# A gated linear attention with a feed-forward layer on one core: outputs and late keys turned by DMA transposes, scores in 64-row tiles

## The chip, the cores and the metric

The kernel runs on one core of one Trainium2 chip. The metric is the device time of that core in microseconds. Eight runs of the kernel before have a median of 205.31 us (204.4 to 206.87).

## The reference

Four batches, eight heads, 768 positions and a head size of 48. With f = sigmoid(f_logit), every head keeps a 48 x 48 state:

```
for t in range(S):
    state = f[:, :, t, :, None] * state + outer(k[:, :, t], v[:, :, t])
    y[:, :, t] = q[:, :, t] @ state
x = y, heads side by side        # 3072 tokens x 384
h = x @ w_in                     # 384 x 2048
out = gelu(h) @ w_out            # 2048 x 384, exact gelu, float32
```

## The kernel before

**Chunks.** The 3072 tokens are cut into 24 chunks of 128 positions, six to a batch. Inside a chunk the decay is turned into factors: Exp and Ln on ACT (L403, L407) give log f, a triangular matmul sums it over positions (L424), and two Exp (L428, L432) give gt and rg. DVE multiplies kp = k * rg (L435) and qp = q * gt (L439), and GpSimd casts v into a padded tile vp (L449). A batch in the sense of the list BATCH is one to four chunks whose Exp and Ln are one instruction.

**Attention of a chunk (`attn`).** `keys` turns kp and qp with four TensorE transposes each into PSUM (L490). Two DVE copies place the keys in kb, a zero-padded tile in which each head of a pair has its own column block, so that a full 128-row matmul can multiply one head's keys with the pair's queries (L230 by way of `copy`); one ACT copy makes qT (L228). `scores` runs eight 128-column matmuls in two halves (L533), and DVE multiplies each half with the causal mask (L541). The state matmul (L581) has 96 columns per pair; DVE and GpSimd update the state (L596, L598, L604). The outputs are made already transposed, with features on partitions: eight matmuls of v against scores (L618) and, if there is a state, four of the state against qT (L622), all 128 columns. Four copies of the shapes 96 x 384 and 3 times 32 x 128 place them in xT, the input of the feed-forward layer. The first four chunks (NDB 2, "dbl") are loaded two at a time with two neighbouring positions on a partition, and have their own views.

**Feed-forward (`ffn_group`).** Chunks are taken in groups (SIZES, four or two chunks). The first layer (L664) uses 16 x 3 matmuls a group with w_in as weights, ACT does Gelu out of PSUM (L668), and the second layer (L681) has 16 matmuls of 384 columns a chunk, in four steps "F2.n.r" of four, step r using the r-th piece of w_out. ACT copies the result (L228) and SP stores it (L689).

**What sets the order.** The code collects all operations in a planner (`Plan`), with an engine, an estimated length, dependencies, ring buffers (`Ring`, `Buf`) and a priority (PRI); the planner places them greedily by earliest start, and the instructions are issued per engine in that order. Each engine works strictly through its list. An operation with an "alt" may go to another engine if its chunk is below ALTN. Loads, stores (and every other DMA of the plan) go through SP's one queue; the weights are cast and loaded through GpSimd's. ORDER fixes how the loads of chunks (c), w_in (W) and w_out (O) follow each other. LOCK and the gates separate Exp stretches from Gelu stretches on ACT, because a change of function table costs a load (L774). PSUM has eight banks: three hps (feed-forward), three aps (attention), two tp (transposes). In the first 26 us, gaps that the planner foresees on PE are filled with dummy matmuls (L755).

Of the kernel before, what the change touches and what calls it, by code (L numbers as in the profile page):

```python
# [8 lines left out]
F32 = mybir.dt.float32  # L9
BF16 = mybir.dt.bfloat16  # L10
# [4 lines left out]
class Ring:  # L15


    def __init__(self, bufs=0, make=None, fixed=None):
        self.bufs, self.make, self.fixed, self.order = bufs or len(fixed), make, fixed, []
        self.zero = None  # L20
# [5 lines left out]
class Buf:  # L26
# [3 lines left out]
    def ready(self):  # L30

        r = self.ring
        if self.slot is not None:
            return 0.0
        if len(r.order) < r.bufs:
            z = r.zero[len(r.order)] if r.zero else None
            return z.vis if z else 0.0
        old = r.order[len(r.order) - r.bufs]
        t = 0.0
        for u in old.users:  # L40
            if u.end is None:
                return None
            t = max(t, u.vis)
        return t
# [6 lines left out]
    def t(self):  # L51
        if self.handle is None:
            r = self.ring
            self.handle = r.fixed[self.slot] if r.fixed else r.make(**self.kw)
        return self.handle
# [10 lines left out]
class Plan:  # L66
# [34 lines left out]
    def run(self):  # L101
# [10 lines left out]
        while left:  # L112
            best, stay, cand = None, None, []
            for o in left:
                ok = True
                t0 = o.nb
                for b in o.bufs:
                    v = b.ready()
                    if v is None:
                        ok = False  # L120
                        break
                    t0 = max(t0, v)
# [41 lines left out]
def kernel(  # L164
# [12 lines left out]
    C = 128  # L177
# [9 lines left out]
    SIZES = [4, 2, 2, 4, 4, 4, 4]  # L187
    ORDER = ['c0', 'c1', 'W0', 'c2', 'c3', 'W1', 'c4', 'W2', 'c5', 'c6', 'W3', 'O0', 'O1', 'O2', 'O3']
# [3 lines left out]
    RMAJOR = 0  # L192
    LOCK = 4
    KBALT = 1
    ALTN = 4
    BIAS = 0
    PRI = {'F': 2, 'RG': 5, 'R': -2, 'GL': 2, 'Tk': 20, 'VC': -10, 'Y': 20, 'x': 2, 'QT': 10, 'C': -2, 'T': 2, 'O': -20, 'A': 2}
    QALTN = 0
    NDB = 2
    CRING = 1  # L200
    CEARLY = 3
    HPB, ASB = 3, 3
    BATCH = [2, 2, 1, 1, 2, 1, 1, 2, 4, 2, 1, 1, 2, 1, 1]
# [5 lines left out]
    ld = ctx.enter_context(tc.tile_pool(name="ld", bufs=6))  # L209
    ld2 = ctx.enter_context(tc.tile_pool(name="ld2", bufs=2))  # L210
    amp = ctx.enter_context(tc.tile_pool(name="amp", bufs=5))
    lg = ctx.enter_context(tc.tile_pool(name="lg", bufs=3))
    el = ctx.enter_context(tc.tile_pool(name="el", bufs=3))
    at = ctx.enter_context(tc.tile_pool(name="at", bufs=3))
    fx = ctx.enter_context(tc.tile_pool(name="fx", bufs=3))
    fg = ctx.enter_context(tc.tile_pool(name="fg", bufs=2))
    hp = ctx.enter_context(tc.tile_pool(name="hp", bufs=HPB, space=PSUM))
    asp = ctx.enter_context(tc.tile_pool(name="asp", bufs=ASB, space=PSUM))
    tpp = ctx.enter_context(tc.tile_pool(name="tpp", bufs=2, space=PSUM))
# [47 lines left out]
    NLF, NQ, NV, NKB = 2, 4, 6, 3  # L267
    lfs = [one.tile([C, 4, H, 64], BF16, name=f"lf{i}") for i in range(NLF)]
    qps = [one.tile([C, H, 64], BF16, name=f"qp{i}") for i in range(NQ)]
    kps = [one.tile([C, H, 64], BF16, name=f"kp{i}") for i in range(NQ)]  # L270
    vps = [one.tile([C, H * VB], BF16, name=f"vp{i}") for i in range(NV)]
    KBW = P2 * 2 * C + 64
    kbs = [one.tile([C, 2 * KBW], BF16, name=f"kb{i}") for i in range(NKB)]
# [27 lines left out]
    r_qp = padded(qps, "POOL", 0.2, zpad, -95)  # L301
    r_kp = padded(kps, "POOL", 0.2, zpad, -95)
    r_vp = padded(vps, "DVE", 0.65, zall, -99)
    r_kb = padded(kbs, "DVE", 1.2, zall, -93)
# [3 lines left out]
    r_fl = Ring(3, lambda: lg.tile([C, 4, H, D], F32, name="fl"))  # L308
    r_in = {n: Ring(6, lambda n=n: ld.tile([C, H, D], F32, name=n)) for n in ("qt", "kt", "vt")}
    r_gt = Ring(3, lambda: el.tile([C, H, D], F32, name="gt"))  # L310
    r_rg = Ring(3, lambda: el.tile([C, H, D], F32, name="rg"))
    r_gl = Ring(3, lambda: el.tile([C, 4, P2], F32, name="gl"))
    r_in2 = {n: Ring(2, lambda n=n: ld2.tile([C, H, 2 * D], F32, name=n + "2")) for n in ("qt", "kt", "vt")}
    r_qT2 = Ring(2, lambda: ld2.tile([C, P2, 2, C], BF16, name="qT2"))
    r_qT = Ring(3, lambda: at.tile([C, P2, C], BF16, name="qT"))
    r_am = Ring(5, lambda: amp.tile([C, 4, C], BF16, name="am"))
    r_rr = Ring(3, lambda: at.tile([C, P2, 2 * D], F32, name="rr"))
    r_tn = Ring(3, lambda: at.tile([C, P2, 2 * D], F32, name="tn"))
    r_xT = Ring(3, lambda: fx.tile([C, KO, 4 * C], BF16, name="xT"))
    r_os = Ring(3, lambda: fx.tile([C, d_model], F32, name="osb"))  # L320
    r_gT = Ring(2, lambda: fg.tile([C, FO * 4 * C], BF16, name="gT"))
    r_hp = Ring(HPB, lambda: hp.tile([C, 512], F32, name="hps"))
    r_as = Ring(ASB, lambda: asp.tile([C, 512], F32, name="aps"))
    r_tp = Ring(2, lambda: tpp.tile([C, P2, C], BF16, name="tp"))
# [26 lines left out]
    X = [{} for _ in range(NCH)]  # L351

# [38 lines left out]
    def stage1(g):  # L391
# [23 lines left out]
        for n in ns:  # L415
# [3 lines left out]
            x.update(qp=r_qp.new(), kp=r_kp.new(), vp=[r_vp.new() for _ in range(1 + dbl)])  # L419
            pr = 10 * n  # L420

            def cum(gps=gps, j=j):
# [13 lines left out]
                x["kp"].t()[:, :, 0:D], loaded(n, "kt"), rg.t(), ALU.mult),  # L436
                rd=[("rg", n), ("kt", n)], wr=[("kp", n)],
                bufs=[x["kp"], x["kt"], rg], prio=pr, name=f"KP{n}")
            P.add("DVE", 0.57, lambda x=x, gt=gt, n=n: eng().tensor_tensor(  # L439
                x["qp"].t()[:, :, 0:D], loaded(n, "qt"), gt.t(), ALU.mult),  # L440
                rd=[("gt", n), ("qt", n)], wr=[("qp", n)],
                bufs=[x["qp"], x["qt"], gt], prio=pr + 1, name=f"QP{n}",
                  alt=(("POOL", 0.9),) if n < QALTN else None)

            for a, vb in enumerate(x["vp"]):
                rows = slice(64 * a, 64 * a + 64) if dbl else slice(0, C)

                def cast(vb=vb, rows=rows, n=n):
                    nc.gpsimd.tensor_copy(vb.t()[rows].rearrange("p (h x) -> p h x", x=VB)[:, :, 0:D],  # L449
                                          loaded(n, "vt")[rows])  # L450
                P.add("POOL", 0.52, cast, rd=[("vt", n)],
                      wr=[("vp", n, a)], bufs=[vb, x["vt"]], prio=pr, name=f"VC{n}")
# [19 lines left out]
    def vwin(vp, h):  # L472
        o = h * VB - D * (h % 2)
        return vp[:, o:o + C]

    def keys(n):

        x, dbl = X[n], n < 2 * NDB
        qp, kp = x["qp"], x["kp"]
        tps = [r_tp.new(), r_tp.new()]  # L480
        kb = x["kb"] = r_kb.new()
        if dbl:
            qT = x["qT"] = X[n - 1]["qT"] if n % 2 else r_qT2.new()
        else:
            qT = x["qT"] = r_qT.new()
        pr = 10 * n

        def trans(i, src):
            for p in range(P2):
                nc.tensor.transpose(tps[i].t()[:, p, :], src.t()[:, 2 * p:2 * p + 2, :], ident)  # L490
        P.add("PE", 0.225, lambda: trans(0, kp), rd=[("kp", n), "ident"], wr=[("tk", n)], bufs=[tps[0], kp],
              prio=pr + 4, name=f"Tk{n}")
        P.add("PE", 0.225, lambda: trans(1, qp), rd=[("qp", n), "ident"], wr=[("tq", n)], bufs=[tps[1], qp],
              prio=pr + 4, name=f"Tq{n}")

        def block(hh):
            src = tps[0].t()[64 * hh:64 * hh + D]
            if dbl:
                w = kb.t()[64 * hh:64 * hh + D].rearrange("q (a x) -> q a x", a=2)[:, :, 0:P2 * 2 * C]
                w = w.rearrange("q a (p h c) -> q a p h c", p=P2, h=2)[:, :, :, hh, 0:64]  # L500
                copy(w, src.rearrange("q p (a c) -> q a p c", a=2))
            else:
                copy(kbv(kb, 0)[64 * hh:64 * hh + D, :, hh, :], src)
        for hh in range(2):
            P.add("DVE", 0.42, lambda hh=hh: block(hh),
                  rd=[("tk", n)], wr=[("kb", n, hh)], bufs=[tps[0], kb],
                  prio=pr + 4, name=f"KB{n}", alt=(("ACT", 0.6),) if KBALT and n < ALTN else None)
        P.add("ACT", 0.6, lambda: copy(qT.t()[:, :, n % 2, :] if dbl else qT.t(), tps[1].t()),
              rd=[("tq", n)], wr=[("qT", n)], bufs=[tps[1], qT], prio=pr + 4, name=f"QT{n}",
              alt=(("DVE", 0.42),) if n < ALTN else None)  # L510

    def kbv(kb, a):
        return kb.t()[:, a * P2 * 2 * C:(a + 1) * P2 * 2 * C].rearrange("q (p h c) -> q p h c", p=P2, h=2)

    def scores(n):
# [4 lines left out]
        qT = X[n]["qT"]  # L520
        ams = [[None] * two for _ in range(2)]
        for m in range(n, n + two):
            X[m]["ams"] = ams
        for half in range(2):
            for i in range(two):
                ap_, am, kb = r_as.new(), r_am.new(), X[n + i]["kb"]
                ams[half][i] = am

                def amm(half=half, ap_=ap_, kb=kb):
                    for e in range(4):  # L530
                        p, hh = 2 * half + e // 2, e % 2
                        for a in range(two):
# [281 lines left out]
```

## Time and profile before

| what | value |
|---|---|
| median of 8 runs | 205.31 us |
| the profiled execution, its time | 206.87 us |
| its span, first to last instruction | 205.1 us |
| mean granted TensorE clock | 0.983 |
| first-layer matmuls (L664) / second-layer (L681) | 336 / 384 |
| attention: scores (L533) / outputs (L618 and L622) / transposes (L490) | 224 / 224 and 80 / 192 |
| Gelu on ACT (L668) | 96 of 598 ns |
| mask multiply on DVE (L541) | 48 of 686 ns |
| kb copies on DVE (L230) / qT copies on ACT (L228) | 45 of 419 ns / 23 of 596 ns |
| output copies on DVE: 96 x 384 / 32 x 128 | 21 of 554 ns / 67 of 288 ns |
| DMA moved | 27.03 MB |

A page of the profile gives busy time per engine, the span in 40 slices (tenths busy), the waits and the costliest groups of instructions. PE is TensorE's matmul stream and PEld its weight loads, which overlap it. A matmul's record lasts longer than its share of the stream, because matmuls are pipelined; what a block of matmuls costs is read from its start to the start of the next block. "A <- B: 2.4, 1, 2.4" means that A stood 2.4 us in all for B, once, 2.4 us at longest. SPq is the queue in which SP issues DMAs, one after the other.

### The profile page before, as it was taken

The page shows a single profiled execution, that of the slowest core. Times are in us where ns is not written, and L with a number is a line of the kernel's source. Part 1 is how long each engine was busy: PE and PEld are TensorE (multiplying, and loading weights), DVE is VectorE, ACT ScalarE, POOL GpSimd, SP SyncE. Part 2 cuts the span into 40 slices and gives each one's busy share as a digit, 9 for nine tenths or more (in the row PEclk, how much of TensorE's full clock was granted, in tenths as well). Part 3 has the DMA queues.
Part 4 walks back from the last instruction along what each step waited for, and adds up shares of the span by engine and source line. Part 5 has one row for each costly group of instructions (what it writes and reads, how often), then busy time and mean ns, then how long its engine had stood idle before and what let it go on. Part 6 is the DMA issues. An engine that isn't in the chain of part 4 may idle for free.

```text
span 205.1 us, 4638 instructions
## 1 busy us (share of the span) xinstructions
PE 190.6 (93%) x1787; PEld 130.5 (64%) x1787; DVE 122.6 (60%) x263; ACT 140.0 (68%) x257; POOL 58.2 (28%) x131
## 2 busy tenths in 40 slices
PE   6799788995999999987999999999999999999992
PEld 6699575452678779765666677746676565644561
DVE  7767888150299579488999579965289961000000
ACT  3584955975458878979876975787978674169410
POOL 7983939300024313311453103220032200000000
PEclk9789999997899999999999999999999999999999
DMA  6999999997299997999989998100121000220022
GB/s 162 262 253 185 167 202 181 189 184 112 63 211 216 196 229 162 220 190 205 198 171 198 189 239 176 38 0 3 38 77 43 0 0 6 73 77 0 3 77 77
DMA packets 98773, 27.03 MB, mean 132 GB/s; under 512 B 92096, under 2 KB 98752, under 8 KB 98752
## 3 DMA queue, kind: packets, MB, share of 16 engines
q1 hardware_dynamic: 94976, 23.60, 54.0%
q0 software_dynamic: 3776, 3.15, 9.8%
q8 instruction: 14, 0.23, 0.5%
q14 instruction: 7, 0.06, 0.1%
HBM read 25.17 MB, written 4.72 MB: 146 GB/s over the span
## 4 chain that ended last, share of the span: by engine, by line
PE 68%; DMA 12%; ACT 7%; DVE 5%; issue 3%; POOL 2%; SPq 2%; ACTq 0%; POOLq 0%
PE hps L681 28%; PE hps L664 22%; DMA wout<-in_moe_w_out_dram 6%; DMA fl<-in_f_logit_dram 4%; PE aps L533 4%; PE aps L618 4%; PE tp L490 4%; PE hps L755 2%; DMA vt<-in_v_dram 2%; ACT lf L407 1%; PE aps L581 1%; ACT fl L403 1%; ACT xT L228 1%; PE aps L622 1%; DVE kp L435 1%
## 5 line engine op out<-in xcount | busy, mean ns | idle before, releaser
L681 PE MATMUL hps<-wout,gT 128*128 128x384 bf16 x384 | 69.6, 331 | 2.4 <-DMA wout<-in_moe_w_out_dram 2.4
L664 PE MATMUL hps<-xT,win 128*128 128x512 bf16 (+1 forms) x336 | 68.8, 349 | 0.0
L668 ACT ACTIVATE gT<-hps 128x512 bf16<-128x512 f32 x96 | 56.0, 598 | 15.3 <-PE hps L664 12.5
L681 PEld LDWEIGHTS <-gT 128*128 128x128 bf16 x384 | 36.8, 99 | 25.6 <-issue 4.3
L664 PEld LDWEIGHTS <-win 128*128 128x128 bf16 x336 | 31.3, 98 | 22.0
L541 DVE TENSOR_TENSOR am<-aps,mask 128x512 bf16<-128x512 f32 x48 | 31.1, 686 | 11.8 <-PE aps L533 11.2
L230 DVE CAST xT<-aps 32x128 bf16<-32x128 f32 (+1 forms) x88 | 30.9, 351 | 8.2 <-PE aps L622 4.7
L228 ACT ACTIVATE osb<-hps 128x384 f32<-128x384 f32 x22 | 10.8, 489 | 24.5 <-PE hps L681 24.1
L449 POOL CAST vp<-vt 128x384 bf16<-128x384 f32 (+1 forms) x28 | 16.0, 572 | 38.6 <-DMA vt<-in_v_dram 32.2
L439 DVE TENSOR_TENSOR qp<-qt,gt 128x384 bf16<-128x384 f32 x24 | 14.0, 582 | 20.6 <-ACT gt L428 20.4
L598 POOL TENSOR_TENSOR tn<-rr,gl 128x384 f32<-128x384 f32 x16 | 13.2, 826 | 38.9 <-DVE rr L596 17.3
L618 PE MATMUL aps<-am,vp 128*128 128x128 bf16 x224 | 20.9, 219 | 0.5 <-ACT rg L432 0.4
L230 DVE COPY kb<-tp 48x512 bf16<-48x512 bf16 x45 | 18.9, 419 | 3.7 <-ACT kb L228 2.2
L604 POOL CAST sb<-tn 48x192 bf16<-48x192 f32 x40 | 14.2, 355 | 23.9 <-DVE tn L592 20.0
L618 PEld LDWEIGHTS <-vp 128*128 128x128 bf16 x224 | 17.1, 98 | 4.5 <-issue 0.9
L533 PE MATMUL aps<-qT,kb 128*128 128x128 bf16 x224 | 17.9, 219 | 1.4 <-DVE kb L230 0.9
L533 PEld LDWEIGHTS <-kb 128*128 128x128 bf16 x224 | 14.7, 98 | 5.6 <-DVE kb L230 1.1
L228 ACT ACTIVATE qT<-tp 128x512 bf16<-128x512 bf16 x23 | 13.7, 596 | 4.1 <-PE tp L490 3.9
L774 ACT ACT_TABLE_LOAD x12 | 15.4, 1283 | 0.9 <-PEq L798 0.7
L622 PE MATMUL aps<-qT,sb 128*128 128x128 bf16 x80 | 15.3, 219 | 0.0
L435 DVE TENSOR_TENSOR kp<-kt,rg 128x384 bf16<-128x384 f32 x24 | 13.5, 571 | 0.2
L428 ACT ACTIVATE gt<-aps 128x384 f32<-128x384 f32 x19 | 9.4, 493 | 5.5 <-PE aps L424 5.3
(55 smaller groups left out, 172.2 us busy)
## 6 DMA issues: line engine op xcount, KB each, us to landing
out_dram<-osb SPq DMA_DIRECT2D x24, 192.0 KB, 1.9
fl<-in_f_logit_dram SPq DMA_DIRECT2D x20, 192.0 KB, 3.8
kt<-in_k_dram SPq DMA_DIRECT2D x20, 192.0 KB, 3.8
qt<-in_q_dram SPq DMA_DIRECT2D x20, 192.0 KB, 3.7
vt<-in_v_dram SPq DMA_DIRECT2D x20, 192.0 KB, 3.9
wout<-in_moe_w_out_dram POOLq DMA_DIRECT2D x4, 384.0 KB, 11.6
win<-in_moe_w_in_dram POOLq DMA_DIRECT2D x4, 288.0 KB, 6.0
fl<-in_f_logit_dram SPq DMA_DIRECT2D x2, 384.0 KB, 4.9
```

Of the source, the lines that this page charges most:

```text
L228: nc.scalar.activation(dst, src, AF.Copy)
L230: nc.vector.tensor_copy(dst, src)
L435: P.add("DVE", 0.57, lambda x=x, rg=rg, n=n: nc.vector.tensor_tensor(x["kp"].t()[:, :, 0:D], loaded(n, "kt"), rg.t(), ALU.mult), rd=[("rg" ...
L449: nc.gpsimd.tensor_copy(vb.t()[rows].rearrange("p (h x) -> p h x", x=VB)[:, :, 0:D], loaded(n, "vt")[rows])
L533: nc.tensor.matmul(ap_.t()[:, e * C:(e + 1) * C], kbv(kb, a)[:, p, hh, :], qT.t()[:, p, :, 64 * a:64 * a + 64] if dbl else qT.t()[:, p, :] ...
L541: nc.vector.tensor_tensor(am.t(), ap_.t().rearrange("p (h t) -> p h t", t=C), mk.unsqueeze(1).to_broadcast([C, 4, C]), ALU.mult)
L618: nc.tensor.matmul(yp.t()[:, p * C:(p + 1) * C], vwin(vp.t(), 2 * p + hh), ams[half][i].t()[:, 2 * (p % 2) + hh, :], start=(hh == 0 and i ...
L622: nc.tensor.matmul(yp.t()[:, p * C:(p + 1) * C], osb.t()[:, p, :], queries(p), start=False, stop=True)
L664: nc.tensor.matmul(hps.t()[:, i * tok:(i + 1) * tok], win[:, kk, fo * 128:(fo + 1) * 128], xT.t()[:, kk, 0:tok], start=(kk == 0), stop=(kk ...
L668: acts.append(P.add("ACT", 0.6, lambda u=u, hps=hps: nc.scalar.activation(view()[:, u * pk:(u + 1) * pk, :].rearrange("p a b -> p (a b)"), ...
L681: nc.tensor.matmul(op.t()[:, 0:d_model], view()[:, fo, s_ * C:(s_ + 1) * C], wout[:, fo, :], start=(fo == 0), stop=(fo == FO - 1))
L774: nc.scalar.preload_act_table_set("natural_log_exp_and_others" if table == "exp" else "gelu_and_others")
```

## The change

- **Keys and queries share tiles.** kp and qp lie in one tile kqp; both sets of transposes go to one PSUM tile and one copy (DVE, or ACT) makes kq. There is no padded kb any more for these chunks (the kb path stays in the code but no chunk takes it, since ROWN is 20 and NT 16).
- **Scores in 64-row tiles.** Each head of a pair has its own 64 partitions of kq; the matmuls of the two heads alternate between the two row halves of the array and write two PSUM banks, both taken by one operation.
- **From chunk 16 on (NT)** the TensorE transposes and the copy are replaced by one DMA transpose of kqp (128 x 1024, bf16) issued from SP.
- **From chunk 8 on (NY)** the outputs come with positions on partitions: four matmuls of 96 columns (queries as weights, state moving) and eight of 48 columns (scores as weights, v moving). Two copies write yt, and a DMA transpose (128 x 384, bf16) from SP writes xT.
- **First four chunks:** one v tile and one cast each in place of two, 64-row and 64 x 64 tiles in the matmuls.
- **Planning:** groups [4, 2, 4, 2, 4, 4, 4], other batches, loads in another order (W0 first, W1 after c5), other priorities, alternatives up to chunk 11, LOCK 12, RMAJOR 1 (the first group's second layer goes by piece of w_out across the chunks), and rings whose buffers are fixed by slot.

```diff
-    SIZES = [4, 2, 2, 4, 4, 4, 4]
-    ORDER = ['c0', 'c1', 'W0', 'c2', 'c3', 'W1', 'c4', 'W2', 'c5', 'c6', 'W3', 'O0', 'O1', 'O2', 'O3']
+    SIZES = [4, 2, 4, 2, 4, 4, 4]
+    ORDER = ['W0', 'c0', 'c1', 'c2', 'c3', 'c4', 'c5', 'W1', 'W2', 'c6', 'W3', 'c7', 'O0', 'O1', 'O2', 'O3']
...
-    RMAJOR = 0
-    LOCK = 4
-    ALTN = 4
-    BIAS = 0
+    RMAJOR = 1
+    LOCK = 12
+    ALTN = 12
+    BIAS = 0.2
...
+    ROWN = 20
+    NT = 16
+    NY = 8
...
-    BATCH = [2, 2, 1, 1, 2, 1, 1, 2, 4, 2, 1, 1, 2, 1, 1]
+    BATCH = [2, 2, 2, 1, 2, 1, 2, 4, 2, 2, 2, 2]
...
+        if n >= NT:
+            def xbar():
+                return nc.sync.dma_start_transpose(out=kq.t().rearrange("q i p t -> q (i p) t"),
+                                                   in_=kqp.t().rearrange("t i h d -> t (i h d)"))
+            P.add("DMA", 1.0, xbar, rd=[("kp", n), ("qp", n)], wr=[("kq", n)], bufs=[kqp, kq],
+                  prio=-10, name=f"KT{n}").lat = 3.0
+            return
...
+            P.add("DVE", 0.70, lambda: copy(kq.t()[:, :, :, n % 2, :] if dbl else kq.t(), tp.t()),
+                  rd=[("tk", n), ("tq", n)], wr=[("kq", n)], bufs=[tp, kq], prio=pr + 4, name=f"KQ{n}",
+                  alt=(("ACT", 1.02),))
...
+        for i in range(two):
+            aps = [r_as.new(), r_as.new()]
+
+            def amm(i=i, aps=aps):
+                for p in range(P2):
+                    for a in range(two):
+                        for hh in range(2):
+                            rows = slice(64 * hh, 64 * hh + 64)
...
+                            nc.tensor.matmul(aps[hh].t()[half if dbl else slice(0, C), p * C:(p + 1) * C],
+                                             t[rows, 0, p, i, half] if dbl else t[rows, 0, p, :],
+                                             t[rows, 1, p, :, half] if dbl else t[rows, 1, p, :],
+                                             start=True, stop=True)
...
+        if n >= NY:
+            def ytok():
+                for p in range(P2):
+                    if c > 0:
+                        nc.tensor.matmul(yp.t()[:, 96 * p:96 * p + 96], kq.t()[:, 1, p, :], osb.t()[:, p, 0:96],
+                                         start=(p == 0), stop=False, skip_group_check=True)
+                for p in range(P2):
+                    for hh in range(2):
+                        h = 2 * p + hh
+                        nc.tensor.matmul(yp.t()[:, D * h:D * h + D], ams[hh][0].t()[:, p, :],
+                                         vps_[0].t()[:, h * VB:h * VB + D],
+                                         start=(c == 0 and h == 0), stop=(h == H - 1), skip_group_check=True)
...
+            yt = r_yt.new()
+            for i, (d0, d1, f0, f1) in enumerate(((0, 96, 0, 288), (96, 128, 288, 384))):
+                P.add("DVE", (0.43, 0.23)[i], lambda d0=d0, d1=d1, f0=f0, f1=f1: copy(
+                    yt.t()[:, :, d0:d1], yp.t()[:, f0:f1].rearrange("t (k e) -> t k e", k=KO)),
+                    rd=[("yp", n)], wr=[("yt", n, i)], bufs=[yp, yt], prio=pr + 2, name=f"X{n}",
+                    alt=(("ACT", (0.42, 0.26)[i]),) if n < ALTN else None)
+
+            def xbar():
+                return nc.sync.dma_start_transpose(out=xT.t()[:, j], in_=yt.t().rearrange("t k e -> t (k e)"))
+            P.add("DMA", 0.8, xbar, rd=[("yt", n, 0), ("yt", n, 1)], wr=[("x", n, i) for i in range(4)],
+                  bufs=[yt, xT], prio=-10, name=f"XT{n}").lat = 3.0
+            return
```

## The prediction

> **What bounds the kernel now.** I read the page's busy shares and slices first, then a table by stage, then PE's waits, then PE's instructions in order of time.
>
> ```profile
> PE 190.6 (93%) x1787; PEld 130.5 (64%) x1787; DVE 122.6 (60%) x263; ACT 140.0 (68%) x257; POOL 58.2 (28%) x131
> ...
> PE   6799788995999999987999999999999999999992
> ...
> DVE  7767888150299579488999579965289961000000
> ...
> PEclk9789999997899999999999999999999999999999
> ```
>
> The table by stage (length, then busy us of PE, weight load, DVE, ACT, POOL, then granted clock, DMA share, GB/s):
>
> ```profile
> 0.00:33.00 33.00, 26.71 (x390) 24.14 (x391) 25.96 (x52) 19.36 (x41) 23.32 (x66) 0.95 1.04 204
> 33.00:50.00 17.00, 14.64 (x97) 7.79 (x95) 6.41 (x15) 13.61 (x21) 5.00 (x8) 0.97 1.16 176
> 50.00:90.00 40.00, 40.00 (x401) 30.62 (x400) 26.49 (x57) 29.12 (x54) 10.89 (x21) 0.97 0.84 179
> 90.00:97.00 7.00, 4.98 (x67) 3.62 (x65) 6.14 (x15) 6.64 (x13) 0.51 (x1) 1.00 1.00 206
> 97.00:170.00 73.00, 72.89 (x664) 47.20 (x662) 57.55 (x127) 56.91 (x106) 18.46 (x36) 1.00 0.45 97
> ```
>
> The reader sees PE with no gap from 50 to 170 us, except 2.0 us in 90:97. After 170 come only the last feed-forward matmuls. So from 50 us on a microsecond of PE work removed is a microsecond of span removed; a microsecond of DVE or ACT work is not. Before 33 us PE's business is partly filler matmuls (L755). The waits of PE and the place of the longest:
>
> ```profile
> PE hps L681 <- DMA wout<-in_moe_w_out_dram: 2.4, 1, 2.4
> ```
>
> ```profile
> 45.26 1.46 PE L681 MATMUL hps<-wout,gT 128*128 128x384 bf16 x8
> 49.08 5.02 PE L681 MATMUL hps<-wout,gT 128*128 128x384 bf16 x20 [2.36 <-DMA wout<-in_moe_w_out_dram]
> ```
>
> PE ran the two first steps of one output chunk, then stood 2.36 us for the third piece of w_out. The stand also cooled its clock (0.76 granted in 50 to 55 us): 20 matmuls of 384 columns took some 4.9 us where 64 of them take 10.4 us later, that is 3.25 us. The stall thus cost 2.4 + 1.7 = 4.1 us.
>
> The prices of attention work on PE come from start to next start:
>
> ```profile
> 92.77 0.54 PE L459 MATMUL aps<-negcol,lf 128*128 128x1 bf16 x16
> 93.17 0.32 PE L424 MATMUL aps<-lf,trin 128*128 128x384 bf16 x1
> ...
> 105.76 0.28 PE L618 MATMUL aps<-am,vp 128*128 128x128 bf16 x2
> ...
> 106.43 0.81 PE L664 MATMUL hps<-xT,win 128*128 128x512 bf16 x3
> ...
> 107.08 0.61 PE L533 MATMUL aps<-qT,kb 128*128 128x128 bf16 x8
> 107.53 0.39 PE L490 MATMUL tp<-ident,kp 128*128 128x128 bf16 x4
> 107.75 1.46 PE L664 MATMUL hps<-xT,win 128*128 128x512 bf16 x6
> 109.05 0.33 PE L581 MATMUL aps<-vp,kp 128*128 128x96 bf16 x4
> 109.22 0.81 PE L664 MATMUL hps<-xT,win 128*128 128x512 bf16 x3
> ```
>
> So per chunk: outputs (8 of L618 and 4 of L622) 0.67 us, scores 0.45, the two sets of transposes 2 x 0.22, 96-column matmuls 0.042 each, one-column matmuls 0.40/16 = 0.025 each, all with 128-column weights.
>
> **The change part by part.**
>
> *Keys and queries by DMA, chunks 16 to 23.* Removed from PE: 8 x 0.445 = 3.6 us, all in the dense stage.
>
> *Outputs with positions on partitions, chunks 8 to 23.* Removed: 14 chunks with a state at 0.67 and two (12 and 18) without at 0.45: 10.3 us. Added: 4 matmuls of 96 columns (0.17) and 8 of 48. The trace has no 48-column matmul; it lies between the one-column pace (0.025, so 0.20) and the 96-column pace (0.042, so 0.34). I take the middle, 0.27. That gives 0.44 with a state, 0.27 without, 6.7 us in sum: 3.6 saved, bounds 2.5 and 4.7.
>
> *Scores in 64-row tiles, chunks 4 to 23.* Before, 8 matmuls of 128 rows, 0.45. After, 8 of 64 rows that alternate between the array's upper and lower half and two PSUM banks. The trace has no tiled matmul. If pairs run together the 8 take four slots, 0.22. The rule that speaks against it is in the Trainium skill, "TensorEngine Tiling (Array Packing)", section Key Properties: a change of tiling mode, not only of tile, drains the engine. A drain can be sized by the row: a 128-column matmul's record lasts 0.219 and the next starts after 0.056, so about 0.16 of tail is normally hidden. Two drains around four slots make 0.22 + 0.33 = 0.55; two drains and no pairing 0.78. By the row alone the 20 chunks save 20 x 0.23 = 4.5 us, with the rule they lose 20 x 0.10 = 2.0. I take 0.55, a loss of 2.0, because each chunk's scores stand alone between full-height matmuls; bounds -4.5 and +6.6. The four first chunks (64x64 tiles, 32 matmuls a pair as before) are put at nothing: PE has filler there.
>
> *Key and query copies.* Before, two kb copies of 0.42 (DVE) and one qT of 0.60 (ACT) a chunk. After, one copy of both. By 0.42 for 512 and about 0.15 fixed I estimate 0.7 on DVE, near 1.0 on ACT; none from chunk 16 on. Output copies fall from 0.55 + 3 x 0.29 = 1.42 to two copies of about 0.66. DVE falls by 0.9 a chunk from 8 on and by 1.6 from 16 on, hidden behind PE in the dense stages: nothing in the sum. If that cover were absent it would be a gain.
>
> *First 50 us.* Nothing in the span can be gained here unless w_out is met in time. In the new order the first group's second layer goes by w_out piece over three open chunks (RMAJOR 1): the first two pieces then give PE 3 x 2 x 0.65 = 3.9 us of work instead of 1.3. The 2.6 us more cover the 2.36 us stand. I take the whole 4.1 us, bounds 0 (three accumulators hold all three hps banks, so the first layer of the next group cannot fill) and -4.1. The stretch before it: fewer memsets (two small kb tiles in place of three of 0.97 us) and copies speed the attention of the first chunks, some 1.5 us. Putting W0 ahead of c0 moves about 0.3 MB at 204 GB/s, 1.4 us, in front of the first f load, on which all waits; its two issues also take POOL 0.64 us each among the constants. Sum 0, bounds -3 and +2.
>
> *Order and locks.* Group sizes, batches and priorities move whole operations but add no PE work; LOCK 12 keeps Exp and Gelu apart only for the last group. That can add ACT table loads (now 12 of 1.28 us, 15.4 us). ACT has 16 us free in 97:170, so I put this at nothing and its risk into the waits below; PE would wait for Gelu if ACT's cover were gone.
>
> *The 2.0 us idle at 90 to 97.* PE waits there for Exp and Ln of a batch of four; the new batches still hold a four. I count -0.5, between 0 and -2.
>
> *The transposes as DMAs and their waits.* 16 of 98 KB and 8 of 262 KB are issued from SP, in order with loads and stores. The nearest rows:
>
> ```profile
> SPq L689 <- ACT osb L228: 86.0, 16, 16.7
> ```
>
> ```profile
> kt<-in_k_dram SPq DMA_DIRECT2D x20, 192.0 KB, 3.8
> ```
>
> SP stands for output rows before it issues stores; what is queued behind waits too. A transpose held for its copy likewise holds the loads, and the loads' readers. Six buffers per input are ahead of that. By the row, DMA passes 200 GB/s, so 0.5 and 1.3 us of transfer, 4 us to landing: hidden, since PE has other groups' matmuls. The Trainium skill disagrees with itself: "Advanced Engine Details and Errata", X-Bar Transpose (TRN2), has transposes as fast as other DMAs, which is the row; "VectorE: DVE Perf Modes", The three transpose paths, gives 1309 ns for one 128x128 block, so an estimate of 3 x 1.31 = 3.9 and 8 x 1.31 = 10.5 us if blocks follow each other. By the first the sum gets nothing; by the second a late chunk needs 14.4 us of transposes against 6.6 us of PE work. I take the row, since one small transfer by itself is mostly latency (kt lands after 3.8 us but is followed by another each us). Where the key copies' stall goes: next late can be the transposed keys, or the scores' two PSUM banks, now needed at once out of three, with first- and second-layer matmuls queued behind on PE. For these waits I add 1.5 us, bounds 0 and 4.
>
> Sum: -3.6 - 3.6 + 2.0 - 4.1 + 0 - 0.5 + 1.5 = -8.3. The profiled execution took 206.9 us, span 205.1 and 1.8 around it; it would become 198.6. The median of the runs, 205.3, is 1.6 lower, so the median after is 197.0.
>
> **Rivals.**
> 1. *PE's saving happens, but new waits take it* (16%). For: PE is one queue, three banks, SP one queue. Against: PE hardly ever waits from 97 us on. The 4.1 us of w_out stay and waits are at 4: -8.3 + 4.1 + 2.5 = -1.7, 203.6.
> 2. *Transposes follow block by block* (21%), the slower side. Place: chunks 16 to 23, where 11 blocks a chunk pass one stream while PE needs 5.2 + 1.4 = 6.6 us. It decides from 6.6/11 = 0.6 us a block. At 0.75 us: (8.25 - 6.6) x 8 = 13.2 us later, less 8.3: 210.2; at the page's 1.31 far more. For: no transpose is in the trace, and loads share the DMA engines to 128 us. Against: the DMA share falls to 0.45 over 97:170.
> 3. *Score tiles pair without drains* (8%): 0.22 instead of 0.55, 6.5 us less: 190.5.
> My forecast holds 55%.
>
> **How the numbers follow.** A difference under 0.5%, about 1 us, can't be told from no change. The forecast's own spread is 193 to 201; rival 3 lies below, 2 above. The range 191 to 208 leaves out the lower half of rival 3 and the most of rival 2 above its mild cases. Faster by over 0.5%: the forecast, rival 3 and most of rival 1, 0.73. Same: the rest of rival 1, 0.06. Slower: 0.21.
>
> **What would show it.** Right: no L490-like transposes from chunk 16 on; 48-column matmuls at 0.025 to 0.042 pace; score blocks about 0.55 from start to the next work; no wait of PE for w_out near 46 us and a clock of 1.0 at 50; transposes landing within about 4 us. Wrong: PE waiting for xT, kq or aps after 97 us; SP issues of a transpose lasting several us; loads ending well after 128 us; score blocks near 0.8; a w_out wait that comes back.

## The result, and the profile after

The changed kernel takes 202.56 us (median of 19 runs, 198.58 to 205.01) where the one before takes 205.44 beside it (56 runs): ratio 0.9763, interval 0.9725 to 0.9802. That is faster, by 2.0 to 2.8%, and inside the range, with less gain than the 4% forecast. On another chip it took 198.9 (6 runs, 197.84 to 199.71) against 204.87: ratio 0.9705, 0.9669 to 0.974. Medians here are over all runs, while a ratio takes only runs within 1.5% of their kernel's fastest: of these 19 runs five, median 200.67, and the profiled one is not among them. The profiled execution took 203.92 us, span 201.9; that of the other chip, called the control below, 198.36 and 196.4.

The page, as before: busy time, then slices.

```profile
PE 184.6 (91%) x1730; PEld 116.1 (57%) x1730; DVE 94.6 (47%) x186; ACT 130.5 (65%) x234; POOL 56.4 (28%) x123
...
PE   6799793999999999999999992989999999999993
...
DVE  6468467574177607601699972442068740000000
...
PEclk9999999799999999999999997599999999999999
```

The table by stage, columns as before:

```profile
33.00:50.00 17.00, 15.91 (x120) 8.60 (x121) 11.03 (x23) 11.41 (x22) 7.92 (x14) 0.90 1.07 187
...
90.00:97.00 7.00, 6.78 (x42) 3.97 (x41) 0.56 (x1) 5.78 (x7) 1.02 (x2) 1.00 0.96 191
97.00:170.00 73.00, 67.58 (x648) 40.66 (x647) 43.30 (x86) 50.29 (x91) 18.54 (x36) 0.95 0.77 155
```

PE lost 6 us of busy time, DVE 28. The gaps at 45 and 90 us are gone, and two new ones stand in PE's row: the seventh slice (about 30 to 35 us) and the 25th (about 121 to 126), each with a lowered clock beside it. The dense stage, full before, now has 5.4 us without PE work.

PE in order of time through that place (start, length of the group, idle before it and its releaser):

```profile
120.57 0.34 PE L598 MATMUL aps<-vp,kqp 128*128 128x96 bf16 x4
124.84 1.44 PE L719 MATMUL hps<-xT,win 128*128 128x512 bf16 x3 [3.93 <-issue]
...
127.39 2.74 PE L719 MATMUL hps<-xT,win 128*128 128x512 bf16 x6
...
135.32 0.40 PE L546 MATMUL aps<-kq 64*128 64x128 bf16 x8 [0.81 <-DMA kq<-kqp]
```

The first layer of group 4 (chunks 12 to 15) stands 3.93 us. The page names no releaser; in the control the same stand, 2.04 us, is put down to the transpose into xT. Then six L719 take some 2.6 us where six took 1.3 (granted clock 0.50 over 125 to 130), about 2.7 us lost in all: 6.6 us at one place. SP's queue over the same time (start, time that SP is held by the issue):

```profile
114.08 1.34 SPq L654 DMA_TRANSPOSE xT<-yt  x1
115.52 1.25 SPq L494 DMA_TRANSPOSE kq<-kqp  x1
...
118.11 1.25 SPq L396 DMA_DIRECT2D qt<-in_q_dram  x1
119.46 1.54 SPq L494 DMA_TRANSPOSE kq<-kqp  x1
121.10 2.50 SPq L654 DMA_TRANSPOSE xT<-yt  x2
```

The copies that the last two transposes read, on DVE:

```profile
115.35 0.61 DVE L239 CAST yt<-aps 128x288 bf16<-128x288 f32 x2
116.94 0.62 DVE L239 CAST yt<-aps 128x288 bf16<-128x288 f32 x2 [0.98 <-PE aps L639]
```

They had ended by 117.6, but the transposes were issued only at 121.10, behind two key transposes and three loads. Once issued they are quick: PE goes on 3.7 us after the first of them was issued. From issue to landing, the time of the issue included, the page's DMA part says (median us last):

```profile
xT<-yt SPq DMA_TRANSPOSE x16, 2.8
kq<-kqp SPq DMA_TRANSPOSE x8, 3.1
```

### The profile page after: what moved, and what is told of

Read it like the earlier page. It is cut to its first block, busy times and chain, and to the rows that moved or that the text cites. A ratio compares the mean times of both kernels' runs of the same rounds, so it can differ in the third digit from the quotient of the medians.

```text
span 201.9 us, 4467 instructions
## 1 busy us (share of the span) xinstructions
PE 184.6 (91%) x1730; PEld 116.1 (57%) x1730; DVE 94.6 (47%) x186; ACT 130.5 (65%) x234; POOL 56.4 (28%) x123
## 4 chain that ended last, share of the span: by engine, by line
PE 69%; DMA 10%; SPq 9%; ACT 4%; DVE 3%; issue 2%; POOL 1%; DVEq 0%; ACTq 0%; POOLq 0%
PE hps L719 30%; PE hps L736 27%; DMA fl<-in_f_logit_dram 7%; SPq L386 4%; PE aps L546 3%; SPq L396 3%; PE tp L502 2%; DMA kq<-kqp 2%; PE aps L639 1%; SPq L392 1%; DMA xT<-yt 1%; PE aps L634 1%; PE aps L432 1%; PE aps L598 1%; ACT fl L411 1%
## 5 line engine op out<-in xcount | busy, mean ns | idle before, releaser
L719 PE MATMUL hps<-xT,win 128*128 128x512 bf16 (+1 forms) x336 | 72.3, 361 | 4.5 <-issue 3.9
L736 PE MATMUL hps<-wout,gT 128*128 128x384 bf16 x384 | 67.0, 326 | 0.0
L736 PEld LDWEIGHTS <-gT 128*128 128x128 bf16 x384 | 36.6, 98 | 23.1
L719 PEld LDWEIGHTS <-win 128*128 128x128 bf16 x336 | 31.3, 99 | 30.4 <-issue 7.3
L443 DVE TENSOR_TENSOR kqp<-kt,rg 128x384 bf16<-128x384 f32 x24 | 15.2, 633 | 26.6 <-ACT rg L440 26.6
L454 POOL CAST vp<-vt 128x384 bf16<-128x384 f32 x24 | 13.1, 550 | 45.2 <-DMA vt<-in_v_dram 37.2
L411 ACT ACTIVATE fl<-fl 128x768 f32<-128x768 f32 (+2 forms) x12 | 10.1, 843 | 9.1 <-DMA fl<-in_f_logit_dram 9.0
L239 DVE CAST yt<-aps 128x288 bf16<-128x288 f32 (+1 forms) x28 | 9.3, 366 | 12.5 <-PE aps L639 11.3
L447 DVE TENSOR_TENSOR kqp<-qt,gt 128x384 bf16<-128x384 f32 x24 | 14.2, 590 | 0.0
L546 PE MATMUL aps<-kq 64*128 64x128 bf16 (+1 forms) x224 | 10.0, 225 | 3.3 <-DVE kq L239 2.4
L502 PE MATMUL tp<-ident,kqp 128*128 128x128 bf16 x128 | 12.4, 229 | 0.3 <-DVE kqp L443 0.2
L810 PE MATMUL hps<-trin 128*128 128x128 bf16 x118 | 10.6, 258 | 1.7 <-POOL trin L260 1.6
L502 PEld LDWEIGHTS <-kqp 128*128 128x128 bf16 x128 | 9.0, 104 | 4.7 <-issue 1.3
L239 DVE CAST xT<-aps 32x128 bf16<-32x128 f32 (+1 forms) x20 | 7.2, 361 | 8.8 <-ACT xT L237 3.8
```

The source lines that it names most:

```text
L239: nc.vector.tensor_copy(dst, src)
L443: P.add("DVE", 0.57, lambda x=x, rg=rg, n=n: nc.vector.tensor_tensor(x["kqp"].t()[:, 0, :, 0:D], loaded(n, "kt"), rg.t(), ALU.mult), rd=[( ...
L502: nc.tensor.transpose(tp.t()[:, i, p, :], kqp.t()[:, i, 2 * p:2 * p + 2, :], ident)
L546: nc.tensor.matmul(aps[hh].t()[half if dbl else slice(0, C), p * C:(p + 1) * C], t[rows, 0, p, i, half] if dbl else t[rows, 0, p, :], t[ro ...
L719: nc.tensor.matmul(hps.t()[:, i * tok:(i + 1) * tok], win[:, kk, fo * 128:(fo + 1) * 128], xT.t()[:, 0:s, kk, :], start=(kk == 0), stop=(k ...
L736: nc.tensor.matmul(op.t()[:, 0:d_model], view()[:, fo, s_ * C:(s_ + 1) * C], wout[:, fo, :], start=(fo == 0), stop=(fo == FO - 1))
```

## The experiments

The theory, Q in the expectations: SP's in-order queue sets when xT and kq arrive. A transpose holds SP 1.25 to 1.3 us (median 1.298 for xT), a load 0.4 to 0.65 when the queue is free; from 104 to 145 us SP goes from one issue to the next without rest. The rival D: transposes are slow transfers that contend with loads in the DMA engines. The two can mix: a load at 111.88 holds SP for 2.10 us, and no run tells why. Runs 2 to 5, 7 and 8 let the kernel's planner order everything anew, so each has stands of its own; runs 1, 6 and 9 to 12 keep the plan and differ from the changed kernel only in what is shown.

**1. Three loads later in SP's order.**

```diff
+    P.placed.sort(key=lambda o: (o.start + (5.0 if o.name in ("ldf20", "ldkt20", "ldqt20") else 0.0), o.seq))
```

> The same instructions in the same order on every engine but SP's queue: the loads of f, k and q of chunk 20 are issued behind the output transposes of chunks 14 and 15 instead of ahead of them. Theory Q (SP's single queue is what made PE stand 3.9 us near 121 us): the three loads' issue, 2.6 us, leaves the front of those transposes, so the stand falls from 3.9 to about 1.3 us and the cooled clock after it mostly goes; 3 to 5 us below the changed kernel, 196 to 199.5. Rival D (the transposes are late because they move slowly among the loads on the DMA engines): the stand stays near 3.9 us, time as the changed kernel, 200.5 to 202.5.

Measured 201.69 us (6 runs), ratio 0.9643 (0.9587 to 0.9699); profiled span 201.4. SP and PE in that profile:

```profile
118.71 2.52 SPq L654 DMA_TRANSPOSE xT<-yt  x2
```

```profile
123.22 0.82 PE L719 MATMUL hps<-xT,win 128*128 128x512 bf16 x3 [1.48 <-DMA xT<-yt]
...
129.16 0.40 PE L546 MATMUL aps<-kq 64*128 64x128 bf16 x8 [3.02 <-DMA kq<-kqp]
```

With only SP's order changed, the pair is issued 2.5 us behind the start of its first copy in place of 5.75, and the stand falls from 3.93 to 1.48. But PE now stands 3.02 us for chunk 18's keys, with the clock at 0.66 over 130 to 135. Their transpose:

```profile
123.39 2.39 SPq L494 DMA_TRANSPOSE kq<-kqp  x1
```

and the landings of this run's eight key transposes:

```profile
DMA to landing us min/median/max: 3.0/3.2/5.7
```

It landed only at about 129.1, 5.7 us after its issue; at the median of 3.2 it would have been there at 126.6, and PE had waited since 126.14. So the first stand follows the order of the queue, while most of the second is a slow landing, which is D's theory. The times don't decide either: two of the six (197.74 and 198.76, on which alone the ratio rests) are in Q's range, the median is in D's.

**2 to 4. Fewer DMA transposes:** keys and queries by PE (run 2), outputs as before (3), neither by DMA (4).

```diff
-    ROWN = 20
-    NT = 16
-    NY = 8
+    ROWN = 24   # runs 2, 4
+    NT = 24     # runs 2, 4
+    NY = 24     # runs 3, 4
```

> Keys and queries of chunks 16 to 23 turned by TensorE as before; output transposes stay. The plan is made anew. Theory Q: PE gets 3.6 us more work, SP is freed of 8 issues of 1.25 us, so the stand near 121 us shrinks below 1 us: 198.5 to 201.5. Rival D: the output transposes still run among loads, the stand stays and 3.6 us of PE work come on top: 204 to 206.

> Outputs of all chunks made transposed by TensorE as before; key transposes by DMA stay. Both theories: no first-layer matmul waits for a DMA, PE has 4.5 us more work than in the changed kernel, and the stand of 3.9 us with its 2.7 us of cooled clock is gone: 199.5 to 202. If the rest of the gain comes from the new planning alone, it is no slower than the changed kernel.

> No DMA transpose at all: keys, queries and outputs as before, scores in 64-row tiles, the new groups, order and priorities. PE has 3.6 + 4.5 = 8.1 us more work than in the changed kernel and none of its 6.6 us loss near 121 us: 201 to 204. If the new planning and the missing w_out stand are worth 4 us by themselves, it is about 201; if they are worth nothing, 205.

Measured: run 2 206.73 us (0.9986, 0.9944 to 1.0029), run 3 208.03 (1.0101, 1.0062 to 1.0139), run 4 206.8 (203.14 to 207.73, no interval). Q's numbers for runs 2 and 3 missed. Run 2 stands 4.67 us for xT all the same, as D had it:

```profile
122.59 1.21 SPq L654 DMA_TRANSPOSE xT<-yt  x1
```

```profile
127.82 1.44 PE L719 MATMUL hps<-xT,win 128*128 128x512 bf16 x3 [4.67 <-DMA xT<-yt]
```

This transpose took 5.2 us to land (median of the 16: 2.8), so about half of that stand is a slow landing. Run 3 has no late transpose but waits 2.43 us for DVE's copies of the outputs at 124 us. With no transposes PE is busy 190.9 us, as before the change. Runs 2 and 3, each without one kind of DMA transpose, are thus no faster than the kernel before; run 4 is not settled (203.14 once, else 206.6 and more). How much of the 4 to 5 us is the new plan is not separated.

**5. Run 4, with scores on padded copies as before from chunk 4 on.**

```diff
-    ROWN = 24
+    ROWN = 4
```

> As the run without DMA transposes (206.8 us), and also the scores of chunks 4 to 23 through padded kb tiles and full-height matmuls as before; to be compared with that run. If tiled scores cost PE what full-height ones do (0.43 against 0.45 us a chunk), the two are within 1 us: 206 to 208, ACT and DVE having 0.7 us more copies a chunk. If each score block costs two drains (0.55 us), the padded form is 2 us faster: 204 to 205.5.

Measured 209.94 us, ratio 1.0271 (1.0206 to 1.0335), above both forecasts. It is 3.1 us above run 4, which ran on another chip and stood 0.6% above its own before by the medians. DVE is busy 118.3 us instead of 108.4, and PE's waits for DVE's xT copies are 5.0 us (L662 2.6, L719 2.4) where run 4 has 1.4. The tiled scores thus seem to help, and by the waits more through the copies they save than through PE; both plans were made anew, so what is the plan's part is not shown.

**6. Output rows stored from ACT's queue, not SP's.**

```diff
-nc.sync.dma_start(out=out[n * C:(n + 1) * C, :], in_=osb.t())
+nc.scalar.dma_start(out=out[n * C:(n + 1) * C, :], in_=osb.t())
```

> The changed kernel with the same plan and the same order on PE, DVE and GpSimd; only the 24 output stores are issued by ACT instead of SP. Theory Q (SP's single queue is too full and stands for ACT's results): SP is freed of about 5 us of stores and waits between 95 and 124 us, the transposes of chunks 14 and 15 go out earlier, PE's stand near 121 us falls to 0 to 2.5 us: 197.5 to 200.5. Rival D (transposes are slow on the DMA engines): the stand stays near 3.9 us, 200.5 to 203.

Measured 198.36 us, ratio 0.969 (0.9646 to 0.9734). The stand is still 2.82 us: the pair is issued 3.5 us behind its first copy's start, and PE goes on only 4.9 us after that issue (3.7 and 3.8 in the first profile and the control). The time is not told apart from the control's 0.9705.

**7. The new operations under the old plan:** group sizes, load order, piece order, lock, alternatives, bias, priorities and batches of before, and CEARLY 3 for 4.

```diff
-    RMAJOR = 1
-    LOCK = 12
-    ALTN = 12
+    RMAJOR = 0
+    LOCK = 4
+    ALTN = 4
...
```

> The new operations (DMA transposes, outputs by positions, tiled scores) with the old kernel's groups, order of loads, batches, priorities, locks and piece order of the second layer. If the operations carry the gain, PE has 8 us less work than the kernel before and the w_out stand of 4.1 us comes back, with 2 to 4 us of new waits: 198.5 to 202. If the gain comes from the new planning, 203 to 207.

Measured 204.38 us, ratio 0.9972 (0.9945 to 0.9999). PE's work is down (185.3 us busy) and the time nearly the same: stands of 2.21 us at 20 us (vp), 1.68 at 94 and 1.19 at 136 (kq) took the gain. The stand for w_out, expected back with 4.1 us, is 0.47. The operations alone give little without an order that suits them.

**8. The kernel before, with its w_out pieces across the chunks.**

```diff
-    RMAJOR = 0
+    RMAJOR = 1
```

> The kernel before with one constant changed, RMAJOR 1: the first group's second layer by piece of w_out over its chunks. If the stand for w_out is worth 4.1 us (2.4 of wait, 1.7 of cooled clock), 201 to 202.5. If PE then only waits for something else, 204 to 206.

Measured 205.56 us, ratio 1.0089 (1.0053 to 1.0126). The w_out stand is gone: 28 second-layer matmuls begin at 48.14 and the next work at 52.69, where before the next work began at 53.93. It doesn't reach the end: the first layer had begun 1.5 us later behind a stand of 1.98 us for vp, and small waits of 0.2 to 0.6 us follow later.

**9. Stores on ACT as in run 6, and run 1's shift with 6.5 for 5.0.**

> The changed kernel with the same plan on PE, DVE and GpSimd; the output stores issued by ACT, and the loads of f, k and q of chunk 20 behind the transposes up to chunk 18's keys in SP's queue. Theory Q: the output transposes of chunks 14 and 15 go out at once behind their copies, PE's stand near 118 us (2.8 us with the stores on ACT alone) falls below 1 us and the clock does not fall to one half after it: 194.5 to 197. Rival D: a transpose is slow by itself; stand and time stay as with the stores on ACT alone, 197.5 to 199.5.

Measured 199.75 us, ratio 0.973 (0.9686 to 0.9774). PE in its profile:

```profile
118.94 0.81 PE L719 MATMUL hps<-xT,win 128*128 128x512 bf16 x3
...
129.39 0.40 PE L546 MATMUL aps<-kq 64*128 64x128 bf16 x8 [2.69 <-DMA kq<-kqp]
129.72 2.12 PE L719 MATMUL hps<-xT,win 128*128 128x512 bf16 x9
```

SP:

```profile
114.59 2.52 SPq L654 DMA_TRANSPOSE xT<-yt  x2
...
126.20 1.24 SPq L494 DMA_TRANSPOSE kq<-kqp  x1
```

Beside run 6 the kernel differs only in the place of three loads in SP's order, and the xT stand is nought. PE now stands 2.69 us for chunk 19's keys. DVE had written them by 118.6, but six loads and an output transpose went ahead of theirs, which landed 3.1 us after its issue. So here the queue explains both the stand that went and the one that came; the time missed the 194.5 to 197 and is not better than the control's.

Since the changed kernel itself stood 3.93 us once and 2.04 once, run 1's fall alone would be weak. Over the executions of this plan without filler at this place the stand goes with the queue's delay:

| | from the start of the pair's first copy to its issue, us | stand for xT, us |
|---|---|---|
| first profile | 5.75 | 3.93 |
| control | 3.84 | 2.04 |
| run 6 | 3.51 | 2.82 |
| run 1 | 2.52 | 1.48 |
| run 9 | 1.04 | 0 |
| run 12 | 1.05 | 0 |

Run 6 breaks the order, by the slower landing told there.

**10. Sixty filler matmuls in the place of the stand,** to keep the clock up.

```diff
+                for _ in range(60 if g == 4 and u == 0 else 0):
+                    nc.tensor.matmul(hps.t()[:, 0:C], trin2[:, 0], trin2[:, 0], start=True, stop=True)
```

> The changed kernel with 60 dummy matmuls of 128 columns (3.3 us at full clock) directly ahead of the first-layer matmul that stands near 121 us; nothing else. If the stand costs its 3.9 us and the cooled clock after it another 2.7 us, the dummies fit into the stand and save the 2.7: 197.5 to 200.5 beside 200.6 to 202.6 of the changed kernel. If the cooled clock is no cost of the stand, the time stays or rises by up to 1 us.

> The changed kernel again, as a control on the same chip as the other runs of this call: 200 to 203, with one stand near 34 us and one near 121 us.

Measured 199.66 us, ratio 0.9746 (0.9718 to 0.9775); the control (11) 198.9. Filled, then control:

```profile
120.29 3.51 PE L717 MATMUL hps<-trin 128*128 128x128 bf16 x60
124.14 0.81 PE L721 MATMUL hps<-xT,win 128*128 128x512 bf16 x3 [0.34 <-issue]
...
131.76 0.40 PE L546 MATMUL aps<-kq 64*128 64x128 bf16 x8 [0.47 <-DMA kq<-kqp]
```

```profile
120.73 0.81 PE L719 MATMUL hps<-xT,win 128*128 128x512 bf16 x3 [2.04 <-DMA xT<-yt]
...
129.86 0.40 PE L546 MATMUL aps<-kq 64*128 64x128 bf16 x8 [0.43 <-DMA kq<-kqp]
```

The same work takes 7.6 us from start to start with filler (clock 1.00), 9.1 in the control (clock 0.70 over 120 to 125) and 10.5 in the first profile. Less each one's wait for kq (0.47, 0.43, 0.81) these are 7.15, 8.70 and 9.67, so 1.5 and 2.5 us of this stretch are the clock after the stand. The total is not better than the control's: the profiled execution came to the copies of the pair 1.8 us later (114.90 for 113.13), and why is open.

**12. Run 9, and 30 filler matmuls before chunk 4's scores.**

> As the run with stores on ACT and chunk 20's loads put back, and also 30 dummy matmuls (1.7 us) ahead of the scores of chunk 4, where PE stands 1.4 to 2.4 us near 33 us. If the stand there cools the clock (0.68 in 35 to 40 us of the changed kernel), 1 to 1.5 us below that run; if not, the same within 0.5 us.

Measured 200.4 us (196.68 to 203.47), ratio 0.9657 (0.9603 to 0.9711). The early stand is filled and no cooled clock follows it; 2.69 us for keys stay:

```profile
127.58 0.60 PE L548 MATMUL aps<-kq 64*128 64x128 bf16 x8 [2.69 <-DMA kq<-kqp]
128.12 3.29 PE L721 MATMUL hps<-xT,win 128*128 128x512 bf16 x9
```

After this stand the nine matmuls take 3.29 us, and in run 9 after one of the same length 2.12. The clock is 0.71 over 125 to 130 here and 1.00 over 130 to 135 there. So the fall of the clock is not settled by the length of the stand alone. Run 12 holds the lowest single time of all, but its interval overlaps run 9's and the control's and its median is higher: no version is shown to beat the changed kernel.

## Why the prediction was right and wrong, point by point

- **Keys and queries by DMA, -3.6:** right. 128 transposes (L502) stay of 192.
- **Outputs by positions, -3.6:** direction right, undersized. PE in order of time, a chunk with a state:

```profile
66.69 0.33 PE L634 MATMUL aps<-sb,kq 128*128 128x96 bf16 x4
66.86 0.36 PE L639 MATMUL aps<-vp,am 128*128 128x48 bf16 x8
67.07 0.82 PE L719 MATMUL hps<-xT,win 128*128 128x256 bf16 x6
```

From start to start 0.17 + 0.21 = 0.38 us: 48 columns go at the one-column pace of 0.025. 14 x 0.29 + 2 x 0.24 = 4.5 us saved.

- **Score tiles, +2.0:** wrong in sign.

```profile
57.36 1.46 PE L736 MATMUL hps<-wout,gT 128*128 128x384 bf16 x8
58.76 0.40 PE L546 MATMUL aps<-kq 64*128 64x128 bf16 x8
59.09 0.40 PE L502 MATMUL tp<-ident,kqp 128*128 128x128 bf16 x4
```

Eight L736 need 1.30, so about 0.10 is lost at entry (57.36 + 1.30 = 58.66); the eight tiles take 0.33 and nothing is seen at exit. 0.43 us against 0.45: 0.4 saved over 20 chunks. The term that failed is the drain taken from a record's tail, two of 0.16. Pairing is partial: 0.041 a matmul, neither 0.056 nor 0.028.

- **w_out, -4.1:** the stand is gone (L736 runs from 50.02, clock 1.00 over 50 to 55), the gain is not in this profile. A stand of the same size stands earlier:

```profile
34.00 0.40 PE L546 MATMUL aps<-kq 64*128 64x128 bf16 x8 [2.41 <-DVE kq L239]
```

```profile
30.00:35.00 5.00, 1.55 (x20) 0.98 (x19) 3.23 (x8) 4.08 (x10) 1.03 (x2) 0.98 1.20 205
35.00:40.00 5.00, 5.00 (x38) 2.81 (x37) 3.00 (x7) 1.79 (x3) 3.18 (x7) 0.68 0.96 179
```

By 55.8 us PE had issued 32 second-layer matmuls, before 36. The trace reads back so: ACT waits 3.05 us at 29.84 for chunk 6's f, issued at 22.92 and landed some 6.9 us later, while W1 and W2, issued from 23.54 to 26.99, were loading beside it; xT copies stand behind that on ACT, and DVE's kq copy behind them. This chain is read, not tried: no run changed the load order. In the control L736 starts at 47.99, so it kept about 2 us of the 4.1. The 0 for the stretch before w_out was too kind, and by this reading the load order's price fell between 29 and 40 us.

- **The gap at 90, -0.5:** 0.2 us of 2.0 are left, so -1.8.
- **New waits, +1.5:** the main error. They are 6.6 at 121 us and 0.8 at 135. The step that failed: "hidden, since PE has other groups' matmuls", by which "the sum gets nothing". It priced the transfer and its landing (about 4 us; measured 2.8 and 3.1) but not the time that an issue holds the queue: 24 transposes x 1.28 = 31 us of SP, in a queue that in the profile before already went from load to load without rest from 97 to 115 us. Runs 1 and 9 show that the order in this queue sets the stand at 121 us; in both another transpose was late instead, and neither time is told apart from the control's. The prediction's own list, "SP issues of a transpose lasting several us", looked at the right engine for a held copy, not for a full queue.
- **Rivals:** blocks one after the other (2) is false: three blocks land in 2.8 us and eight in 3.1, where 1.31 a block would give 3.9 and 10.5. D is not needed for the first profile's stand, but it is not refuted: single transposes took 5.2 us in run 2 and 5.7 in run 1. What slowed them is open. Undrained pairs (3) are half true. Rival 1 has the mechanism that is nearest: waits did take most of PE's saving.

Sum for the profiled span: -3.6 - 4.5 - 0.4 + 0 - 1.8 + 6.6 + 0.8 = -2.9; measured 205.1 to 201.9, -3.2. The control's 196.4 is nearly the 196.8 that the forecast implies, by other terms: smaller stands (2.04 and 0.43, with less cooled clock) and 2 us more kept at w_out; that agreement is luck. Why its runs scatter by 6.4 us on the first chips (before: 4.1), by 1.9 on the control's, and run 12's by 6.8 there, stays open, and so does the share of planning in runs 2 to 5. The clock after a like stand, 1.2 us apart in runs 9 and 12, may be one part of the scatter.

## What to carry to other kernels

Price a DMA in three parts: its transfer, its landing, and the time its issue holds the queue. Add the last over the busy stage and see whether the queue still has rest, for a late issue looks like a slow transfer. The two can be told apart: compare the start of the issue with the end of what the DMA reads, then the landing with the issue. When one stand is removed from an in-order plan, name the next operation in that queue: in run 9 xT's wait became kq's, at about the same size. A PE stand of 2 us or more mostly cost clock too (in run 9 not), so a stand's price is to be read until the clock is full again.

## What was not expected of the hardware

- A transpose by DMA holds SP as long for 128x384 as for 128x1024 (1.3 and 1.25 us) and landed 2.3 to 4.9 us after its issue in the first profile, 5.7 at most in run 1.
- Entry into 64-row tiles cost about 0.10 us, the way back nothing to be seen; a paired 64x128 matmul of 128 columns took 0.041 us.
- Stands of 2.0 and 2.4 us were followed by a granted clock of 0.70 and 0.68 over the next 5 us; of 2.8 (run 6) and 3.9 us, by 0.50; one of 2.7 us in run 9 by 1.00. Filler kept it at 1.00.
